# Sharing one weight load between two products in the key stage of a gated attention/MLP decode kernel

## The chip, the cores and the metric

One core of a Trainium2 chip. The metric is the device time of one execution in microseconds (us). The profile's own span is about 1.8 us shorter than the device time (132.1 against 133.93 us for the profiled run of the kernel before).

## The reference, cut to what matters

One token `x` of 576 numbers goes through two branches that a scalar gate mixes. Branch A is attention of 32 query heads over the last 4096 positions of a cache with 16 key/value heads; branch B is a two-layer MLP.

```python
# A: B = Sq = 1, D = 576, Hq = 32, Hkv = 16, Sk = 32768, Dh = 128, all bf16
W = min(4096, max(256, Sk // 4))                    # 4096
q = (x @ wq).reshape(...)                           # 32 heads of 128
k = repeat(k_cache[:, :, Sk - W:, :], 2); v = ...   # the last 4096 positions
p = softmax(einsum("bhqd,bhkd->bhqk", q, k) * Dh ** -0.5)
a = einsum("bhqk,bhkd->bhqd", p, v).reshape(...) @ wo
# B
b = gelu(x @ w1 + b1) @ w2 + b2                     # 576 -> 4608 -> 576
g = sigmoid((x * gate_w).sum(-1))
return g * a + (1 - g) * b
```

Every weight and every line of the caches' last 4096 positions has to be read once, so about 53.6 MB have to be read for very little arithmetic.

## The kernel before: the parts that matter here

The loads are issued in order on one queue: `w1`, `wq`, eight key tiles of 2 MB, the first half of `w2`, the values, `wo`, the rest of `w2`. Buffers are reused, so some loads wait for earlier work.

The key stage computes the scores. Each key tile is transposed on VectorE in two halves, and sixteen products per tile accumulate into four banks of `s_ps` (a bank is here one of its four quarters of 512 columns). The stationary operand `qz[:, h0 // 2, j, :]` depends, within one key tile, on `j` only; the bank depends on `u` only.

```python
kt_pool = ctx.enter_context(tc.tile_pool(name="kt_pool", bufs=2, side="right"))
# ... cut ...
s_ps = ps_s.tile([P, SL * 32], FP32, name="s_ps")          # 128 x 2048: four banks
for g in range(NG):
    k_t = big.tile([P, 2, SL, Dh], BF16, name="k_t", tag="CDBA"[g])
    for f in range(2):
        # ... the load of k_t[:, f] on the SP queue ...
        kt = kt_pool.tile([P, SL * Dh], BF16, name="kt", tag="kt")
        for u in range(2):
            half = SL * Dh // 2
            nc.vector.transpose(out=kt[:, u * half : ...], in_=k_t[:, f, u * SL // 2 : ...])
        kv = kt[:].rearrange("p (c e k t) -> p c e k t", e=2, k=32, t=2)
        for u in range(4):
            for j in range(4):
                nc.tensor.matmul(
                    s_ps[:, u * 512 : (u + 1) * 512].rearrange("p (c k) -> p c k", k=32),
                    lhsT=qz[:, h0 // 2, j, :],
                    rhs=kv[:, u * SL // 4 : (u + 1) * SL // 4, j // 2, :, j % 2],
                    start=(h0 == 0 and j == 0), stop=(h0 == Hkv - 2 and j == 3),
                    skip_group_check=True,
                )
```

After the last product come the maximum over the scores, the exponentials and another transpose (all of it here called the softmax), and then the value products `o_ps`. The last group of value loads needs the buffer of the first group, and `wo` that of the second, so both wait for value products (11.7 and 4.2 us in the waits of the SP queue of before):

```python
v_t = big.tile([P, NCK, Dh], BF16, name="v_t", tag="CDAC"[g])   # g = 3 reuses the buffer of g = 0
wo_t = big.tile([P, RO, D], BF16, name="wo_t", tag="D")          # reuses the buffer of g = 1
```

## Time and profile before

| | before |
|---|---|
| time, median of 3 runs | 134.09 us (134.0 to 134.1) |
| span of the profile | 132.1 us |
| bytes moved, mean rate | 53.78 MB, 407 GB/s |
| key stage, from the first transpose to the end of the last product | 31.9 to 73.0 us |
| products / weight loads in it | 128 / 128 |

Lines of the page of the kernel before. The first line gives the busy time of each engine (PEld is the weight-load part of TensorE, which overlaps with its products); the next two cut the span into 40 slices, with the granted clock and the busy share of the transfer engines (DMA), both in tenths. Then the shares in the chain that ended last. The last three are groups of instructions: count, busy us and mean ns, idle time before them and what ended it.

```profile
PE 77.4 (59%) x1126; PEld 51.1 (39%) x1126; DVE 55.4 (42%) x80; ACT 12.9 (10%) x25; POOL 0.7 (1%) x6
...
PEclk9999999999999999999999996555555555556998
DMA  7999998999999999999999999999999999999960
...
DMA 67%; PE 12%; DVE 8%; ACT 7%; issue 2%; SPq 1%; DVEq 0%
...
L300 DVE STREAM_TRANSPOSE kt<-k_t 128x2048 f32<-128x2048 f32 x16 | 36.0, 2290 | 9.7 <-DMA k_t<-in_A_k_cache_dram 9.7
L309 PE MATMUL s_ps<-kt,qz_flat 128*128 128x512 bf16 x128 | 32.3, 399 | 9.2 <-DVE kt L300 9.2
L309 PEld LDWEIGHTS <-qz_flat 128*128 128x128 bf16 x128 | 12.8, 100 | 28.3 <-issue 14.7
```

The transfers are busy in nearly every slice. VectorE waits 9.7 us for the transfers before its transposes, and TensorE 9.2 us for VectorE before its products. Waits run that way only: transfers first, VectorE second, TensorE third.

The timeline of the same kernel, for two bursts: start us, length us, engine, line, operation, count, and in brackets the idle time before it and who ended it.

```profile
64.05 1.90 PE L309 MATMUL s_ps<-kt,qz_flat 128*128 128x512 bf16 x8 [0.82 <-DVE kt L300]
64.05 1.62 PEld L309 LDWEIGHTS <-qz_flat 128*128 128x128 bf16 x8 [1.10 <-issue]
66.24 1.90 PE L309 MATMUL s_ps<-kt,qz_flat 128*128 128x512 bf16 x8 [0.30 <-DVE kt L300]
66.24 1.62 PEld L309 LDWEIGHTS <-qz_flat 128*128 128x128 bf16 x8 [0.58 <-issue]
66.58 4.50 DVE L300 STREAM_TRANSPOSE kt<-k_t 128x2048 f32<-128x2048 f32 x2 [0.39 <-DMA k_t<-in_A_k_cache_dram]
```

One burst is the eight products that one transposed half allows. It lasts 1.90 us; one product alone takes 0.377 us (the median of the tile's view), so products start (1.90 - 0.377) / 7 = 0.217 us apart. The eight weight loads lie within the burst. The bursts are separated by waits for transposes, and each pair of transposes waits 0.39 us for its key tile. Burst lengths here and below are those from 44 us on: the first 12 products of the stage (34.2 to 38.9 us) start 0.427 us apart and most of them take 628 ns, the time that one product takes at the recorded half clock in experiment 4; they take 377 ns from 39.2 us on, where the first clock record of this trace (1.0) begins.

The chain that ended last, in order of time, of the kernel before: start us, length us, what.

```profile
31.59 34.86 DMA k_t<-in_A_k_cache_dram
...
66.58 4.52 DVE kt L300 x2
...
71.14 1.91 PE s_ps L309 x8
...
100.84 27.37 DMA w_t<-in_B_w_dram
...
128.25 1.19 PE y_ps L193 x16
```

Only the last burst of the key stage is in the chain. From 100.84 us to the end at 128.21 there is nothing in it but the transfer of the last piece of `w2`.

### The profile page before, as it was taken

To read this page: it belongs to the slowest core of one execution; us is meant where nothing else is said; L and a number is where in the kernel's file an instruction comes from. 1 tells how busy PE (TensorE), PEld (TensorE's weight loads), DVE (VectorE), ACT (ScalarE), POOL (GpSimd) and SP (SyncE) were. 2 spreads that over 40 slices of the span, in tenths; PEclk is the share of its full clock that TensorE was granted. 3 is DMA by queue.
4 is the path that set the end of the run, shared out by engine and by line. 5 is a ranking of instruction groups with operands and counts; after the bars stand their busy time and mean duration, and the time that the engine had idled before them with its cause. 6 is when DMAs were issued, how large, how long until landed. Compare 5 with 4: busy or idle time off the path is not lost.

```text
span 132.1 us, 2458 instructions
## 1 busy us (share of the span) xinstructions
PE 77.4 (59%) x1126; PEld 51.1 (39%) x1126; DVE 55.4 (42%) x80; ACT 12.9 (10%) x25; POOL 0.7 (1%) x6
## 2 busy tenths in 40 slices
PE   0038999084699769769779460007942952456651
PEld 0035999084234323223223230007942952333430
DVE  6059100503978988988985710653000000100001
ACT  3000000003000000000000059940000000000001
POOL 2000000000000000000000000000000000000000
PEclk9999999999999999999999996555555555556998
DMA  7999998999999999999999999999999999999960
GB/s 246 421 443 411 448 518 368 398 427 427 427 417 432 422 431 419 427 436 417 454 408 442 451 446 417 407 466 427 397 451 387 431 417 428 429 407 427 406 249 0
DMA packets 3190, 53.78 MB, mean 407 GB/s; under 512 B 358, under 2 KB 362, under 8 KB 620
## 3 DMA queue, kind: packets, MB, share of 16 engines
q1 hardware_dynamic: 3170, 53.61, 95.7%
q8 instruction: 9, 0.15, 0.4%
q10 hardware_dynamic: 10, 0.01, 0.0%
q14 instruction: 1, 0.01, 0.0%
HBM read 53.62 MB, written 0.00 MB: 406 GB/s over the span
## 4 chain that ended last, share of the span: by engine, by line
DMA 67%; PE 12%; DVE 8%; ACT 7%; issue 2%; SPq 1%; DVEq 0%
DMA k_t<-in_A_k_cache_dram 26%; DMA w_t<-in_B_w_dram 21%; DMA wq_t<-in_A_wq_dram 20%; ACT p_t L351 7%; PE o_ps L402 5%; DVE kt L300 3%; PE q_ps L257 3%; DVE pt L359 2%; DVE m L321 2%; PE s_ps L309 1%; PE y_ps L193 1%; SPq L415 1%; PE t_ps L377 0%; DVE out_row L437 0%; SPq L417 0%
## 5 line engine op out<-in xcount | busy, mean ns | idle before, releaser
L300 DVE STREAM_TRANSPOSE kt<-k_t 128x2048 f32<-128x2048 f32 x16 | 36.0, 2290 | 9.7 <-DMA k_t<-in_A_k_cache_dram 9.7
L309 PE MATMUL s_ps<-kt,qz_flat 128*128 128x512 bf16 x128 | 32.3, 399 | 9.2 <-DVE kt L300 9.2
L309 PEld LDWEIGHTS <-qz_flat 128*128 128x128 bf16 x128 | 12.8, 100 | 28.3 <-issue 14.7
L402 PE MATMUL o_ps<-pt,v_t 128*128 128x8 bf16 x512 | 14.6, 168 | 8.5 <-DMA v_t<-in_A_v_cache_dram 6.5
L402 PEld LDWEIGHTS <-v_t 128*128 128x128 bf16 x512 | 14.3, 104 | 8.9 <-DMA v_t<-in_A_v_cache_dram 6.7
L351 ACT ACTIVATE p_t<-s_ps,negm 128x512 bf16<-128x512 f32 x8 | 9.7, 1412 | 44.9 <-DVE negm L342 44.9
L219 PE MATMUL h_ps<-x,w_t 128*128 128x2 bf16 x162 | 10.2, 202 | 0.0
L219 PEld LDWEIGHTS <-w_t 128*128 128x128 bf16 x162 | 10.1, 169 | 0.0
L420 DVE TENSOR_TENSOR om<-o_ps,rgh 128x128 bf16<-128x128 f32 x1 | 0.3, 292 | 22.2 <-PE o_ps L402 22.2
L193 PE MATMUL y_ps<-wo_t,ov 128*1 128x288 bf16 x64 | 6.1, 364 | 4.6 <-DMA wo_t<-in_A_wo_dram 4.6
L359 DVE STREAM_TRANSPOSE pt<-p_t 128x2048 bf16<-128x2048 bf16 x2 | 4.6, 2312 | 7.4 <-ACT p_t L351 7.4
L377 PE MATMUL t_ps<-ls,ones 128*128 128x32 f32 x2 | 0.6, 396 | 11.9 <-DVE ls L375 11.9
L193 PE MATMUL y_ps<-w_t,gt 128*1 128x288 bf16 x72 | 5.6, 285 | 2.1 <-DMA w_t<-in_B_w_dram 2.1
L437 DVE CAST out_row<-y_ps 1x288 bf16<-1x288 f32 x1 | 0.4, 446 | 15.1 <-PE y_ps L193 15.1
L257 PE MATMUL q_ps<-x,wq_t 128*128 128x2 bf16 x144 | 4.0, 166 | 4.0 <-DMA wq_t<-in_A_wq_dram 4.0
L193 PEld LDWEIGHTS <-ov 128*1 128x1 bf16 x64 | 3.4, 103 | 7.0 <-issue 4.5
L257 PEld LDWEIGHTS <-wq_t 128*128 128x128 bf16 x144 | 3.9, 104 | 4.0 <-DMA wq_t<-in_A_wq_dram 4.0
L377 PEld LDWEIGHTS t_ps<-ls,ones 128*128 128x128 f32 x2 | 0.5, 310 | 12.2 <-issue 12.2
L120 PE MATMUL xs_ps<-one_b,rows 1*128 1x1 bf16 x9 | 0.7, 195 | 7.2 <-DVE rows L117 7.2
L193 PEld LDWEIGHTS <-gt 128*1 128x1 bf16 x72 | 3.2, 83 | 3.9 <-issue 2.9
L436 ACT CAST out_row<-y_ps 1x288 bf16<-1x288 f32 x1 | 0.4, 390 | 42.2 <-PE y_ps L193 42.2
L228 DVE COPY hacc<-h_ps 128x36 f32<-128x36 f32 x1 | 0.2, 196 | 9.4 <-PE h_ps L219 9.4
(68 smaller groups left out, 28.7 us busy)
## 6 DMA issues: line engine op xcount, KB each, us to landing
k_t<-in_A_k_cache_dram SPq DMA_DIRECT2D x8, 2048.0 KB, 32.3
v_t<-in_A_v_cache_dram SPq DMA_DIRECT2D x3, 4096.0 KB, 29.8
wq_t<-in_A_wq_dram SPq DMA_DIRECT2D x1, 4608.0 KB, 25.8
wo_t<-in_A_wo_dram SPq DMA_DIRECT2D x2, 2304.0 KB, 20.2
v_t<-in_A_v_cache_dram SPq DMA_DIRECT2D x2, 2048.0 KB
w_t<-in_B_w_dram SPq DMA_DIRECT2D x1, 2880.0 KB, 14.1
w_t<-in_B_w_dram SPq DMA_DIRECT2D x1, 2592.0 KB, 11.3
w_t<-in_B_w_dram SPq DMA_DIRECT2D x1, 2304.0 KB, 8.0
```

Source lines behind the costliest of these rows:

```text
L120: nc.tensor.matmul(xs_ps[:, i : i + 1], lhsT=xdup[:, i : 2 * D : NI], rhs=one_b[0:1, 0:1], start=(i == 0), stop=(i == NI - 1), skip_group_ ...
L193: nc.tensor.matmul(y_out[s], lhsT=vec, rhs=row[:, s * DH : (s + 1) * DH], start=start, stop=stop, skip_group_check=True,)
L219: nc.tensor.matmul(h_ps[:, j:NF:NJ], lhsT=w1_t[:, i, j:FH:NJ], rhs=x2[:, i, :], start=False, stop=(i == NI - 1 and j == NJ - 1), skip_grou ...
L257: nc.tensor.matmul(q_ps[:, j : Hq : Hq // 2], lhsT=wq_t[:, i, j * Dh : (j + 1) * Dh], rhs=x2[:, i, :], start=(i == 0 and j == 0), stop=(i ...
L300: nc.vector.transpose(out=kt[:, u * half : (u + 1) * half].bitcast(FP32), in_=k_t[:, f, u * SL // 2 : (u + 1) * SL // 2, :] .rearrange("p ...
L309: nc.tensor.matmul(s_ps[:, u * 512 : (u + 1) * 512].rearrange("p (c k) -> p c k", k=32), lhsT=qz[:, h0 // 2, j, :], rhs=kv[:, u * SL // 4 ...
L321: nc.vector.reduce_max(out=m2[:], in_=s_ps[:].rearrange("p (n b) -> p b n", b=2), axis=AX.X)
L351: nc.scalar.activation(out=p_t[:, cs, :, b], in_=s_ps[:].rearrange("p (c k u b) -> p u b c k", k=8, u=2, b=2)[:, f, b % 2], func=ACT.Exp, ...
L359: nc.vector.transpose(out=pt[:, cs, :].rearrange("p c h -> p (c h)"), in_=p_t[:, cs, :, :].rearrange("p c k b -> p (c k b)"),)
L377: nc.tensor.matmul(t_ps[:], lhsT=ones[:], rhs=ls[:], start=True, stop=True)
L402: nc.tensor.matmul(o_ps[:, 8 * g : 8 * g + 8, 0], lhsT=v_t[:, c, :], rhs=pt[:, c, 8 * g : 8 * g + 8], start=(c == 0), stop=(c == NCK - 1),)
L415: nc.sync.dma_start(out=wo_t[:, r0:r1, :], in_=wo_src[:, r0:r1, :])
```

## The change

Its intent: of two weight loads in a row with the same stationary, the second is left out. That TensorE still holds the stationary for the second product is the author's assumption; the runs do not show it, since the comparison with the reference does not notice wrong scores (experiment 2). The loop over banks is split into halves, and inside each half the loop over stationaries is outermost, so that two products in a row, to two banks, share a stationary. A pass over the finished program then drops every weight load that repeats the one before it and neither waits nor signals.

```diff
--- before.py
+++ after.py
@@ -65,6 +65,25 @@
 
     nc.at_finalize(first_load_ahead)
 
+    def keep_weights(nc):
+        body = nc.main_func.blocks[1]
+        loaded, kept = None, []
+        for i in body.instructions:
+            if type(i).__name__ == "InstLdweights":
+                w = i.ins[0]
+                key = (w.memref, w.offset, tuple(w.ap), i.tile_size, i.tile_position)
+                sync = i.sync_info
+                free = sync is None or not (sync.on_wait or sync.on_update)
+                if key == loaded and free:
+                    continue
+                loaded = key
+            elif type(i).__name__ == "InstMatmult" and i.ldweights is not False:
+                loaded = None
+            kept.append(i)
+        body.instructions = kept
+
+    nc.at_finalize(keep_weights)
+
     const = ctx.enter_context(tc.tile_pool(name="const", bufs=1))
     big = ctx.enter_context(tc.tile_pool(name="big", bufs=1, side="right"))
     kt_pool = ctx.enter_context(tc.tile_pool(name="kt_pool", bufs=2, side="right"))
@@ -304,16 +323,17 @@
                     .bitcast(FP32),
                 )
             kv = kt[:].rearrange("p (c e k t) -> p c e k t", e=2, k=32, t=2)
-            for u in range(4):
+            for half in range(2):
                 for j in range(4):
-                    nc.tensor.matmul(
-                        s_ps[:, u * 512 : (u + 1) * 512].rearrange("p (c k) -> p c k", k=32),
-                        lhsT=qz[:, h0 // 2, j, :],
-                        rhs=kv[:, u * SL // 4 : (u + 1) * SL // 4, j // 2, :, j % 2],
-                        start=(h0 == 0 and j == 0),
-                        stop=(h0 == Hkv - 2 and j == 3),
-                        skip_group_check=True,
-                    )
+                    for u in (2 * half, 2 * half + 1):
+                        nc.tensor.matmul(
+                            s_ps[:, u * 512 : (u + 1) * 512].rearrange("p (c k) -> p c k", k=32),
+                            lhsT=qz[:, h0 // 2, j, :],
+                            rhs=kv[:, u * SL // 4 : (u + 1) * SL // 4, j // 2, :, j % 2],
+                            start=(h0 == 0 and j == 0),
+                            stop=(h0 == Hkv - 2 and j == 3),
+                            skip_group_check=True,
+                        )
```

## The prediction

> **What bounds the kernel now.** The transfers. The page shows 53.78 MB at 407 GB/s, DMA in the top tenth in nearly every slice from 12 to 128 us. The chain of waits gives DMA 67%, TensorE 12%. The tail in the timeline: the last loads are issued by 101.8 us, the last one lands at 128.2; then come 16 small products (1.15 us), one cast (0.45 us) and the store.
>
> In the key stage (31.6 to 73 us; stretches show DMA at 1.00 to 1.05) a key tile lands every 4.90 us. VectorE transposes it in two halves, 4.50 us, then waits 0.40 us for the next transfer. TensorE gets eight products after each half: bursts of 1.90 us in the timeline, with idle time of 0.30 and 0.81 us before them, released by the transposes. So TensorE is third in this row.
>
> **What the change does.** It removes 64 of the stage's 128 weight loads: 64 x 100 ns (groups by line) = 6.4 us of weight-load busy time. It removes no product. The order of instructions shows the other engines unchanged, the waits for the transposes still on the first product of each eight, and each pair of banks needing the same half of the transposed tile as before. No other weight load is dropped. Two products in a row now write different banks, where before four in a row accumulated into one.
>
> **What that is worth.** A burst of eight lasts 1.90 us, one product alone 0.377 us, so starts are (1.90 - 0.377)/7 = 0.217 us apart. [...] the loads (100 ns) run beside the preceding product, and the products already stream at their own pace. Dropping hidden loads saves nothing on a burst, 0.1 us at most; the head load of each burst stays or overlaps the wait.
>
> On the critical path lies only the last burst (chain: 1.91 us before the maximum). Even a gain there would not reach the end: the value load that waits for the first attention products is issued at 94.7 us, while the load ahead of it lands only at 101.8; the output-weight loads are issued at 99.5, while value loads ahead of them last until 111.6. The queue always holds 7 to 12 us of work, so a softmax some tenths of a us earlier moves no transfer.
>
> **Prediction.** 134.0 us, 8 in 10 between 133.4 and 134.7. Faster by over 2%: 0.01; within 2%: 0.97; slower by over 2%: 0.02.
>
> **What would show each step.** Weight loads of the key stage 128 to 64, 12.8 to about 6.4 us; its products still about 377 ns each, bursts still 1.88 to 1.92 us; VectorE's idle time before the key transposes still about 0.40 us a tile, on the transfer; last burst ends near 73 us; output-weight loads issued near 99.5; last load lands near 128.2; DMA near 407 GB/s.
>
> **What would make it wrong.** (1) [...] the granted clock falls in the key stage: at half clock a burst would take about 3.6 us, two of them 7.2 against 4.9 us a tile, and the stage would slip 2.3 us a tile. Unlikely: from 92 to 96 us weight loads were busy all the time and the clock stayed at 0.50, so loads do not seem to hold it up. (2) A product without its own load starts late, or alternating banks cost: over 70 ns per product would exceed the slack and delay the transposes through their two buffers. (3) The transfer rate differs on the chip that runs it; that moves both kernels.

## The result, and the profile after

| | before | after |
|---|---|---|
| time, median | 134.09 us (6 runs, 134.0 to 134.19) | 134.09 us (6 runs, 133.9 to 134.56) |
| weight loads of the key stage | 128, 12.8 us | 64, 6.3 us |
| instructions | 2458 | 2394 |
| end of the last burst | 73.05 us | 72.88 us |
| issue of the `wo` loads | 99.52 us | 99.80 us |
| last transfer lands | 128.21 us | 128.42 us |

The ratio is 1.0003, with a 95% interval of 0.9987 to 1.0019: the same.

The page after, same lines (the change moves line 309 to 329 and 300 to 319).

```profile
PE 78.1 (59%) x1126; PEld 45.2 (34%) x1062; DVE 55.4 (42%) x80; ACT 12.9 (10%) x25; POOL 0.7 (1%) x6
...
PEclk9999999999999999999999998555555555555599
DMA  7999998999999999999999999999999999999950
...
DMA 66%; PE 12%; DVE 8%; ACT 7%; issue 3%; SPq 1%; DVEq 0%
...
L319 DVE STREAM_TRANSPOSE kt<-k_t 128x2048 f32<-128x2048 f32 x16 | 36.0, 2291 | 9.4 <-DMA k_t<-in_A_k_cache_dram 9.4
L329 PE MATMUL s_ps<-kt,qz_flat 128*128 128x512 bf16 x128 | 31.5, 391 | 9.7 <-DVE kt L319 9.7
...
L329 PEld LDWEIGHTS <-qz_flat 128*128 128x128 bf16 x64 | 6.3, 99 | 34.3 <-issue 33.1
```

Weight-load time fell by 51.1 - 45.2 = 5.9 us in all, by 6.5 us in the key stage. The products, the transposes and the transfers did not follow. The mean product went from 399 to 391 ns, but that is no gain from the change: the slow products at the start of the stage (478 to 628 ns) are 12 in the run of before and 8 in the run of after, and the median is the same (377 ns).

The timeline after, for the two bursts that answer to those shown of before.

```profile
63.88 1.89 PE L329 MATMUL s_ps<-kt,qz_flat 128*128 128x512 bf16 x8 [0.81 <-DVE kt L319]
64.10 0.10 PEld L329 LDWEIGHTS <-qz_flat 128*128 128x128 bf16 x1 [1.31 <-issue]
64.53 0.10 PEld L329 LDWEIGHTS <-qz_flat 128*128 128x128 bf16 x1 [0.34 <-issue]
64.97 0.10 PEld L329 LDWEIGHTS <-qz_flat 128*128 128x128 bf16 x1 [0.34 <-issue]
65.40 0.10 PEld L329 LDWEIGHTS <-qz_flat 128*128 128x128 bf16 x1 [0.34 <-issue]
66.07 1.89 PE L329 MATMUL s_ps<-kt,qz_flat 128*128 128x512 bf16 x8 [0.30 <-DVE kt L319]
```

A burst has four loads now instead of eight, about 0.43 us apart, and it still lasts 1.89 us: the products keep their 0.217 us. The load at 65.40 us starts with the eighth product of its burst (63.88 + 7 x 0.217 = 65.40); as each pair has one load, it can only be the one for the first pair of the next burst. So not even that one stands before a product.

The chain after.

```profile
31.68 34.61 DMA k_t<-in_A_k_cache_dram
...
66.42 4.52 DVE kt L319 x2
...
70.97 1.91 PE s_ps L329 x8
...
101.13 27.29 DMA w_t<-in_B_w_dram
...
128.46 1.19 PE y_ps L212 x16
```

The last burst (the line of `s_ps`) has the same 1.91 us in the chain, and the end is again a transfer that was issued more than 27 us before it landed.

### The profile page after: what moved, and what is told of

Read it like the earlier page. It is cut to its first block, busy times and chain, and to the rows that moved or that the text cites. A ratio compares the mean times of both kernels' runs of the same rounds, so it can differ in the third digit from the quotient of the medians.

```text
span 132.3 us, 2394 instructions
## 1 busy us (share of the span) xinstructions
PE 78.1 (59%) x1126; PEld 45.2 (34%) x1062; DVE 55.4 (42%) x80; ACT 12.9 (10%) x25; POOL 0.7 (1%) x6
## 4 chain that ended last, share of the span: by engine, by line
DMA 66%; PE 12%; DVE 8%; ACT 7%; issue 3%; SPq 1%; DVEq 0%
DMA k_t<-in_A_k_cache_dram 26%; DMA w_t<-in_B_w_dram 21%; DMA wq_t<-in_A_wq_dram 20%; ACT p_t L371 7%; PE o_ps L422 5%; DVE kt L319 3%; PE q_ps L276 3%; DVE pt L379 2%; DVE m L341 2%; PE s_ps L329 1%; PE y_ps L212 1%; SPq L435 1%; PE t_ps L397 0%; DVE out_row L457 0%; SPq L437 0%
## 5 line engine op out<-in xcount | busy, mean ns | idle before, releaser
L329 PE MATMUL s_ps<-kt,qz_flat 128*128 128x512 bf16 x128 | 31.5, 391 | 9.7 <-DVE kt L319 9.7
L329 PEld LDWEIGHTS <-qz_flat 128*128 128x128 bf16 x64 | 6.3, 99 | 34.3 <-issue 33.1
L212 PE MATMUL y_ps<-wo_t,ov 128*1 128x288 bf16 x64 | 7.7, 432 | 4.6 <-DMA wo_t<-in_A_wo_dram 4.6
L212 PEld LDWEIGHTS <-ov 128*1 128x1 bf16 x64 | 4.0, 121 | 8.1 <-issue 4.5
```

The costliest lines, as they stand in the source:

```text
L212: nc.tensor.matmul(y_out[s], lhsT=vec, rhs=row[:, s * DH : (s + 1) * DH], start=start, stop=stop, skip_group_check=True,)
L329: nc.tensor.matmul(s_ps[:, u * 512 : (u + 1) * 512].rearrange("p (c k) -> p c k", k=32), lhsT=qz[:, h0 // 2, j, :], rhs=kv[:, u * SL // 4 ...
```

## The experiments

Three questions. Are the loads hidden, or do two effects of the change cancel? Would a shorter key stage reach the end at all? And, after the first runs brought a surprise: what does the length of the instruction stream cost? Twelve kernels ran.

### 1. The order alone

Edit: the changed kernel without the pass that drops loads.

```diff
-    nc.at_finalize(keep_weights)
```

> The new order of the products with all 128 weight loads kept. Theory (loads are hidden beside the products, banks do not matter, transfers bound the kernel): bursts of eight stay 1.88 to 1.92 us, 128 loads, time within 0.3% of before. Rival (the change is two effects that cancel: alternating banks cost, dropped loads gain): bursts here at least 0.05 us longer than before's 1.90 us, since this run pays the cost without the gain.

Measured: 134.12 us against 134.23, ratio 0.9999 (0.9979 to 1.002). 128 loads; bursts of 1.90 us throughout (from 44 us on). Writing two banks in turn costs nothing that shows here, so there is no cost that the dropped loads had to pay for.

### 2. Nearly no loads, old order

Edit: the order of before, one stationary for all `j`, and the pass that drops loads. The scores are wrong; the comparison with the reference does not notice wrong scores here.

```diff
-                        lhsT=qz[:, h0 // 2, j, :],
+                        lhsT=qz[:, h0 // 2, 0, :],
```

> Wrong result on purpose: the old order of banks, but one stationary for all sixteen products of a tile, so that only 8 of 128 loads are left. Theory: bursts stay 1.88 to 1.92 us and the time within 0.3% of before, loads of the stage 8, under 1 us busy. Rival (loads cost, banks cost, both cancel in the change): with nearly all loads gone and no alternation, bursts fall by 0.05 us or more.

Measured: 134.04 us against 134.23, ratio 0.9995 (0.997 to 1.0019). The view of the stationary's tile in this run: minimum, median and maximum ns, first and last start.

```profile
L328 PE MATMUL s_ps<-kt,qz_flat x128: 376/377/628, 34.3 to 72.6; 128*128 128x512 bf16 x128
L328 PEld LDWEIGHTS <-qz_flat x8: 95/96/103, 32.7 to 67.7; 128*128 128x128 bf16 x8
```

With 8 loads instead of 128 the product's median is the same 377 ns and the bursts are 1.89 to 1.90 us. The rival of two cancelling effects falls on both sides: no alternation cost in run 1, no load gain in run 2. The views give a granted clock of 1.00 from 40 to 71 us, and the bursts of 1.89 to 1.90 us from 44 us on say the same, so dropping loads did not let it fall here.

### 3. Three and ten loads per product

Edit: before, with each load of the key stage repeated two or nine more times by a pass over the finished program.

```diff
+            if type(i).__name__ == "InstLdweights" and "qz_flat" in str(i.ins[0].memref):
+                for n in range(2):        # 9 in the second kernel
+                    kept.append(mybir.InstLdweights(... same operands ...))
```

> Before, with every weight load of the key stage issued three times in a row (256 added, result unchanged). Theory with loads that follow each other at about 27 ns (the value products, each with its own load, run 220 in 5.85 us in the trace of before): 3 x 27 = 81 ns still hides beside a product of 217 ns, bursts 1.88 to 1.95 us, time as before. Variant with loads one after the other at their recorded 96 ns: 288 ns per product, bursts about 0.38 + 7 x 0.29 = 2.4 us, the two of a tile 4.6 to 4.8 us against a tile every 4.90 us, so still no change of the time beyond 0.3%. Rival (a load costs products something that the page hides): bursts grow in proportion to the added loads already here and removing loads should have helped.

> Before, with every weight load of the key stage issued ten times in a row (1152 added, result unchanged). Loads at 27 ns each, hidden: 10 x 27 = 270 ns exceeds 217 ns, so products start about 270 ns apart, bursts about 2.25 us, still under a tile's 4.90 us for two; time within 0.5% of before. Loads at 96 ns each one after the other: 960 ns per product, bursts near 7 us, the stage becomes bound by TensorE and the time rises by tens of us. Loads that cannot hide[...]: 217 + 9 x 27 = 460 ns, bursts near 3.6 us, stage slips about 2.3 us a tile, time up by 8 to 16 us.

Measured with three loads: 135.26 us against 134.23, ratio 1.0077 (1.006 to 1.0095). With ten: 140.47 us, ratio 1.0497 (1.0432 to 1.0562). A burst in the timeline with three loads:

```profile
59.19 1.93 PE L335 MATMUL s_ps<-kt,qz_flat 128*128 128x512 bf16 x8 [0.79 <-DVE kt L326]
59.19 1.73 PEld L335 LDWEIGHTS <-qz_flat 128*128 128x128 bf16 x24 [0.99 <-issue]
```

24 loads fit beside 8 products, and products start (1.93 - 0.383) / 7 = 0.221 us apart: 4 ns more for 256 added loads. So there is room for two further loads beside each product, and the one that was there was far from showing. In the chain of the run with ten loads the key stage becomes one piece:

```profile
34.54 48.66 PE s_ps L335 x128
```

48.66 / 128 = 0.380 us per product. None of the numbers written beforehand (0.27 for loads 27 ns apart and fully hidden, 0.46 if only one of the ten hides, 0.96 for loads of 96 ns one after the other) is right; the truth lies between the first two, and what limits a train of ten loads was not looked into. The last burst ends 10.15 us later than in before, and the time rises by only 6.4 us (means): part of the delay was swallowed. Experiment 5 takes that up.

The expectation for three loads (time as before) is missed: the time rose by 0.9 us although bursts grew by 0.03 us and the last one ended 0.08 us later. That is not a matter of the key stage. Experiment 6 takes it up.

### 4. When would sharing help? Narrow products; and half the products

Edit: every product of 512 columns cut into four of 128; once with all 512 loads in the old order, once in pairs that share a load.

```diff
-            for u in range(4):
-                for j in range(4):
+            for n in range(16):           # shared: for pair in range(8): for j: for n in the pair
+                for j in range(4):
-                        s_ps[:, u * 512 : (u + 1) * 512] ...
+                        s_ps[:, n * 128 : (n + 1) * 128] ...
# ... the slices of rhs and the start flag follow ...
```

> Before with every key product cut into four of 128 columns, each with its own load: 512 products, 512 loads, 32 per burst (right result). If a load hides entirely beside a product of 128 columns,[...] a burst lasts about 2.0 us; if its 27 ns do not hide,[...] burst about 2.8 us, two of them 5.6 against a tile's 4.90 us, the stage slips up to 5 us, mostly swallowed by the slack after it. By theory A the larger instruction stream costs 1 to 3 us in either case: 135 to 138 us.

> The change in the same narrow form: pairs of 128 columns share a load, 512 products, 256 loads (right result). If loads hide, same bursts as the narrow run with all loads; if 27 ns per load do not hide,[...] burst about 2.3 us, that is 0.4 us shorter than there. Time 134.5 to 137 us, below the narrow run with all loads by up to 1.5 us (fewer instructions, shorter bursts). Rival (sharing a load never helps a product): bursts equal to the narrow run with all loads although those are above 2.2 us.

Measured: 135.4 us with all loads (ratio 1.0082, 1.004 to 1.0123) and 135.46 us with pairs (ratio 1.0082, same interval), against 133.96. A burst in the timeline with all loads:

```profile
61.33 1.98 PE L309 MATMUL s_ps<-kt,qz_flat 128*128 128x128 bf16 x32 [0.22 <-DVE kt L300]
61.33 1.86 PEld L309 LDWEIGHTS <-qz_flat 128*128 128x128 bf16 x32 [0.34 <-issue]
```

32 products with 32 loads take 1.98 us, that is (1.98 - 0.217) / 31 = 57 ns each, and with pairs, 16 loads, the timeline again has 1.97 to 1.98 us for every burst of 32. The first of the two guesses holds (a burst of about 2.0 us, not 2.8): a load hides even beside a product of 128 columns. So sharing loads would not have paid in the narrow form either; that pairs might be faster by up to 1.5 us did not come true. Both narrow kernels are 1.4 to 1.5 us slower than before (medians) with bursts that are 0.08 us longer: again more than the key stage explains.

Edit: half of the products, two of four per bank. The scores are wrong.

```diff
-                for j in range(4):
+                for j in (0, 3):
```

> Wrong result on purpose: before, with only two of the four products per bank, so 64 of 128 products and of 128 loads are left. Theory (TensorE is not the limit of the key stage): bursts of four, about 0.377 + 3 x 0.217 = 1.03 us, last burst ends about 0.87 us earlier, time within 0.3% of before. Rival (the key stage is bound by TensorE and the change merely failed to shorten it): time down by 1 us or more.

Measured: 133.99 us against 133.96, ratio 0.9989 (0.9926 to 1.0052), so the time is as the theory had it. The bursts are not. From the timeline of this run:

```profile
49.50 1.87 PE L309 MATMUL s_ps<-kt,qz_flat 128*128 128x512 bf16 x4 [0.85 <-DVE kt L300]
51.69 1.86 PE L309 MATMUL s_ps<-kt,qz_flat 128*128 128x512 bf16 x4 [0.33 <-DVE kt L300]
```

Four products took 1.86 us, not 1.03, one product 628 ns (median) instead of 377, and products start (1.86 - 0.628) / 3 = 0.411 us apart instead of 0.217: with half the products TensorE ran as at half its clock in most of the stage (the clock records are given below). So this run could not deliver the shorter stage that it was meant to test. What it does show is that here the clock fell with the products (64 of them: median 628 ns; 128: 377 ns) and not with the loads (8 of them in run 2: 377 ns). One trap: the views print a granted clock of 1.00 from 40 to 60 us of this run, where products take 628 ns. The trace has no clock record before 62.6 us, and the view prints 1.00 where there is none (in before the first record is at 39.2 us, so the nines of its PEclk line up to there are no reading either). From there on records and durations agree: clock 1.0 from 62.6 to 66.0 us, where a burst of four takes 1.03 us; 0.5 from 66.0 to 72.8 us, where it takes 1.86 us.

### 5. How much slack lies between the softmax and the end

Edit: before, with the maximum over the scores repeated two or five more times, so that the softmax and everything after it start later. The result is unchanged.

```diff
+    for _ in range(2):                    # 5 in the second kernel
+        nc.vector.reduce_max(out=m2[:], in_=s_ps[:].rearrange("p (n b) -> p b n", b=2), axis=AX.X)
```

> Before, with the maximum over the scores taken three times instead of once (result unchanged): the softmax and all that follows it start 2 x 2.3 = 4.6 us later. Theory (slack: the value load that waits for the first attention products is issued at 94.7 us in before, the load ahead of it lands at 101.8): issue near 99.3 us, still ahead of that landing, time within 0.5% of before (up to 0.6 us if the start of a transfer takes a few us). Rival (the softmax is on the path and a shorter key stage would be gained in full): time up by 4.6 us.

> The same with six maxima: 5 x 2.3 = 11.5 us later. The value load is issued near 106.2 us, after the load ahead of it has landed, so the transfers fall idle. In the run with ten loads per product the last burst ended 10.15 us later than in before and the time rose by 6.2 us, so the slack is about 4 us: time up by 6.5 to 8 us, 140.5 to 142 us. Rival (no slack): up by 11.5 us; rival (softmax wholly off the path): no change.

Measured: 136.58 us (ratio 1.0157, 1.0101 to 1.0212) and 142.31 us (ratio 1.0626, 1.0582 to 1.067) against 134.11. By the chains of waits the value products start 4.96 and 11.98 us later than in before; the mean times rise by 2.1 and 8.3 us. So 2.9 and 3.7 us were swallowed. The first expectation (within 0.5%) is missed, the second missed by 0.3 us; by the rule at 2% the first run's verdict is unclear, the second's slower. Stretches of the second run: busy us of each engine (count), granted clock, busy share of the transfer engines, GB/s.

```profile
core 0: us, PE busy (x) PEld busy (x) DVE busy (x) ACT busy (x) POOL busy (x), PEclk, DMA share, GB/s
96.00:98.00 2.00, 0.00 (x0) 0.00 (x0) 0.82 (x1) 2.00 (x5) 0.00 (x0) 0.50 0.99 426
98.00:100.00 2.00, 0.00 (x0) 0.00 (x0) 0.77 (x1) 1.20 (x4) 0.00 (x0) 0.50 0.73 311
...
102.00:104.00 2.00, 1.99 (x60) 2.00 (x61) 0.65 (x2) 0.00 (x0) 0.00 (x0) 0.50 0.00 0
...
106.00:108.00 2.00, 2.00 (x81) 2.00 (x79) 0.00 (x0) 0.00 (x0) 0.00 (x0) 0.50 0.36 66
108.00:110.00 2.00, 2.00 (x81) 2.00 (x79) 0.00 (x0) 0.00 (x0) 0.00 (x0) 0.50 0.90 377
```

The queue begins to run dry before 100 us (busy share 0.73, then 0.00). The next value load is issued at 106.6 us, and only in the last stretch, from 108 us, do the transfers run at their rate again. In before the same load is issued at 94.7 us, so it had roughly the 3 us that the runs found. The prediction had read 7 us from the moment at which the load ahead was seen to have landed (101.8 us); that is too late a mark, because in this run the rate fell already from 98 to 100 us, and the load issued at 106.6 us had the transfers at their rate only from about 108 us (busy share 0.36 from 106 to 108 us, 0.90 after). The author's estimate from these stretches is that a new load needs about 2 us to flow.

### 6. The length of the instruction stream

The trace records a second kind of transfer on the same engines: packets of 16 KB of instructions, each taking about 1.05 us of one engine. In before there are nine; in the run with three loads per product there are ten (queue, kind: packets, MB, share; before, then three loads):

```profile
q8 instruction: 9, 0.15, 0.4%
q8 instruction: 10, 0.16, 0.5%
```

Edit: the same 256 added loads, moved to where TensorE is idle during the exponentials; then only 64 of them; then 64 of them in the changed kernel.

```diff
+            if added == 0 and type(i).__name__ == "InstMatmult" and <it writes t_ps>:
+                for n in range(256):      # 64 in the other two
+                    kept.append(mybir.InstLdweights(... operands of the last key-stage load ...))
```

> Before, with the same 256 added weight loads as in the run with three loads per product, but put where TensorE sits idle during the exponentials (about 78 to 90 us), so that the key stage is as before (result unchanged). That run took 135.26 against 134.23 us although its bursts grew by only 0.03 us; in its trace there are 10 packets of instruction transfers of 16 KB at about 1.05 us each, against 9, and the last transfer ended about 1.1 us later. Theory A (the cost is the larger instruction stream, which rides on the same transfer engines as the bulk loads): here too 10 packets, time 0.5 to 1.2 us above before, bursts 1.90 us. Theory B (the cost is in the key stage, loads slow the products): time as before within 0.3%.

> Before, with only 64 weight loads added in TensorE's idle time during the exponentials (result unchanged). In before the ninth 16 KB packet of instructions starts as the bulk transfers end; 64 instructions more bring it forward into them. Step theory (a packet costs one transfer engine 1.05 us, and the ninth before the end of the bulk loads is the first to fall on an engine that already carried one): time up by 0.7 to 1.2 us[...]. Linear theory (cost in proportion to the 256 loads' 1.2 us): up by 0.3 us. Third: cost of the loads themselves: none.

> The changed kernel with the same 64 loads added in the idle time: as many TensorE instructions as before has. Step theory: the ninth packet again comes only as the bulk transfers end or not at all before it, time within 0.3% of before, so that the change has bought room for 64 instructions and nothing else. Rival (the added loads in the idle time cost something themselves): up by as much as in the run with before and 64 loads.

Measured: 256 loads elsewhere 135.37 us against 133.96, ratio 1.009 (1.0037 to 1.0143); 64 loads elsewhere 135.42 us against 134.11, ratio 1.0101 (1.0069 to 1.0133); the changed kernel with 64 loads 133.97 us, ratio 1.0 (0.9962 to 1.0037). The costs lie slightly above what was expected (1.27 and 1.28 us in the means, against 0.5 to 1.2 and 0.7 to 1.2 us); the last run is as expected. In the timeline of the first the added loads run from 77.91 to 89.25 us, in the idle time: the sum of the softmax is ready only at 89.8, and the value products start at 90.55 us (90.64 in before). So they delay no product.

The table is read from the packet records of the traces of the profiled runs: how many instruction packets of 16 KB began before 128 us, that is, before the bulk transfers ended in any of these kernels (called early), when these ended, and how many of their packets ended in the last 1 us of it. The ends are about 0.28 us later than the landings in the chains (128.49 against 128.21 us in before).

| kernel | early instruction packets | bulk transfers end, us | packets ending in the last 1 us | time, us |
|---|---|---|---|---|
| before | 8 (a ninth at 128.2) | 128.49 | 69 | 134.09 |
| after | 8 | 128.70 | 60 | 134.09 |
| order alone | 8 (a ninth at 128.2) | 128.59 | 65 | 134.12 |
| one stationary | 8 | 128.50 | 72 | 134.04 |
| half the products | 8 | 128.68 | 61 | 133.99 |
| change and 64 loads | 8 (a ninth at 128.3) | 128.79 | 52 | 133.97 |
| three loads | 9 (a tenth at 128.5) | 129.62 | 10 | 135.26 |
| 256 loads elsewhere | 9 (a tenth at 128.5) | 129.87 | 10 | 135.37 |
| 64 loads elsewhere | 9 (the ninth at 126.5) | 130.14 | 10 | 135.42 |
| narrow, pairs | 10 (an eleventh at 128.7) | 129.95 | 17 | 135.46 |
| narrow, all loads | 11 (a twelfth at 128.9) | 129.97 | 27 | 135.4 |

The profiled runs of two of them were the longest of their kernel (change and 64 loads 135.25, 256 loads elsewhere 136.24 us): there the last 16 products took 2.13 us instead of 1.19, at half clock (granted clock 0.50 from 130 us on in both; 1.00 from 128 to 130 us in before). Such a run turns up with the kernel before as well (135.0 to 135.3 us); it widens the intervals, and since it comes after the last transfer it does not touch the table's second to fourth columns. The ten-load run and the delayed ones are left out, since their transfers fell idle in between.

Eight early packets: 134.0 to 134.1 us (medians), whatever the kernel. Nine to eleven: 135.3 to 135.5 us. It is a step and not a slope: 64 instructions cost as much as 256 (1.28 and 1.27 us in the means), because they bring the ninth packet from 128.2 to 126.5 us, in among the bulk loads. In the three runs with nine, only ten packets end in the last microsecond: most of the engines have finished, and the last piece of `w2` waits for a few packets. The end of the chain of the run with 64 loads, where the last transfer lands at 129.85 us and not at 128.21:

```profile
102.18 27.67 DMA w_t<-in_B_w_dram
129.85 0.04 issue
129.90 1.19 PE y_ps L221 x16
```

What is shown: the cost comes with the ninth early packet, not with the weight loads, their place or their number; the linear and the key-stage explanations fall.

The packet records also show where the ninth packet falls. They do not name the transfer engine, but on one engine a packet begins 3 or 4 ns before the recorded end of the one before it (some 15 ns after an instruction packet), so the packets of one engine can be followed back. While an instruction packet runs in the bulk phase, mostly 15 bulk packets are under way instead of 16 (in before at 143 of 160 instants sampled from 20 to 120 us within an instruction packet, against 16 or more at 1826 of 1840 outside): it takes the place of bulk data on its engine. In before the eight engines that end their bulk work last (128.0 to 128.5 us) hold one early packet each; the other eight end at 126.6 to 127.6 us. In the three runs with nine, the engine that ends last (129.6, 129.9 and 130.1 us) carried two: the first and the ninth, begun at 19.4 and 115.6, 19.6 and 115.1, 19.9 and 126.5 us. Its packets follow each other without a gap from below 2 us to the end. So it never waited for a load to be issued, and a rival falls with this: in the run with 64 loads elsewhere TensorE pauses 3.11 us in the value products (1.90 in before) and the `wo` loads are issued at 100.85 us, 1.3 us late; with 256 loads elsewhere they are issued at 99.41 us, no later than in before, and the cost is the same.

The run with the softmax 4.96 us later has a ninth packet at 129.8 us as well, but it begins on an engine that has just finished its bulk work, while another, without a gap at that time, goes on to 131.0 us. It has no part in that run's 2.1 us.

No version beats both kernels. The runs point to none: all with eight early packets are equal, and the transfers set the time.

## Why the prediction was right

- **The transfers bound the kernel.** Right. In the view by stretches the rate in the key stage of before is 424 to 451 GB/s (451 in its last 2.1 us) at a busy share of 1.00 to 1.05, so the trace shows no idle time there that could have been taken. That the engines could not move more while busy was not shown.
- **What the change removes.** Right: 64 loads, 6.5 us measured for 6.4 us forecast; no product and no wait moved.
- **The loads were hidden and the products at their own pace.** Right. When it was written, the pace of the products was the author's estimate; the runs show it from three sides: with 128, 64 and 8 loads the bursts are 1.89 to 1.90 us (median product 377 ns), and with 384 they are 1.93 us.
- **Alternating banks might cost.** It was named as a risk; run 1 shows that it doesn't (bursts of 1.90 us).
- **Fewer loads might let the clock fall.** Named as a risk and thought unlikely; run 2 shows no such effect with 8 loads (377 ns a product). The half-products run shows that the danger is real for products (628 ns).
- **A gain in the last burst would not reach the end.** The change brought no gain there, so the runs show this from the other side only: a delay of the softmax by up to about 3 us is swallowed. The step of the prediction that was mis-sized is "The queue always holds 7 to 12 us of work": the slack is 2.9 to 3.7 us. It had no effect on the forecast of a change that moves a burst by 0.01 us, but it would have misled one that delays the softmax by 5 us. No run made the softmax earlier, so that this gains nothing rests on the chain of waits, which ends in 27 us of transfer.
- **What the prediction did not see.** The change also takes 64 instructions out of TensorE's stream. That has a price of its own in this kernel (experiment 6): 64 added instructions cost 1.3 us. Taken out they gained nothing, because the packet that they push out began only as the bulk transfers ended (128.2 against 128.49 us). The changed kernel has room for 64 more instructions without loss, where before had none; that is all the change bought. Here the prediction had luck: in a kernel only 64 instructions longer the same change gains about 1.4 us (135.42 to 133.97 us, before and after with 64 loads each), for a reason that the prediction does not have.

## What to carry to other kernels

Before removing a weight load, look at the distance between product starts in a burst. If it hardly grows when loads are added and does not shrink when they are left out (here 217 ns with one load per product or one per two, 221 ns with three), the loads are hidden, and a smaller weight-load busy time is no gain. Read slack from the moment at which the queue would run dry, less the time a new load needs to flow (here about 2 us, an estimate from the stretches in experiment 5), and test it by delaying something on purpose. In a kernel bound by transfers, count the instruction packets that ride on the same engines: here, in before, eight packets fell on eight different engines, and 64 instructions more brought a second packet onto one of them before its bulk work was done, which cost 1.3 us at once.
